# One opening, two edits: shorter weight splits on VectorE, and a first image pooled on TensorE with the averaging matrix as the stationary operand

## The chip, the cores and the metric

The kernel runs on one core of one Trainium2 chip. The metric is device time in microseconds (us) for one launch. Before the change it is 2833.58 us, the median of 3 runs (2832.46 to 2833.78).

A core has five engines that each work through their own queue in order: TensorE (PE in the profile; PEld is its weight load), VectorE (DVE), ScalarE (ACT), GpSimd (POOL) and SyncE (SP), which here only issues DMAs. Engines wait for one another through semaphores.

## The reference

```python
kv_pool = kv.reshape(B, H // 4, 4, W // 4, 4, C).mean(axis=(2, 4))   # 4x4 average
kv_flat = kv_pool.reshape(B, -1, C) @ w_sr                           # keys = values
s = (q @ kv_flat.transpose(0, 2, 1)) / np.sqrt(C)
a = np.exp(s - s.max(-1, keepdims=True))
a /= a.sum(-1, keepdims=True) + 1e-09
x = (a @ kv_flat).reshape(B * S, D)
...
h = x @ w_in
g = 0.5 * h * (1.0 + erf(h * inv_sqrt2))
return g @ w_out
```

B is 4, an image has 384 x 32 pixels of C = 128 channels, so 12288 queries and 768 keys per image; `w_in` is 128 x 2048 and `w_out` 2048 x 128. `w_in` and `w_out` come as 8-byte floats, everything else as 4-byte floats.

## The kernel before, in words

**Numbers.** TensorE multiplies in f16, and each f32 operand is split into a high f16 part and a low f16 part. A product then takes three matmuls: high by high, high by low, low by high (L558 to L560, L611 to L613, L424).

**Tiles.** The 49152 queries are 96 tiles of 512, each of 4 chunks of 128. A tile goes through `score` (6 matmuls of 384 columns a chunk), `evac` (VectorE reads the scores out of PSUM and takes the extreme), `exp` (ScalarE), `attn_hi` and `attn_lo` (VectorE makes the two f16 parts), `attn_turn` (a DMA transpose), `av` (18 matmuls), `x_out`, then 16 pairs of `mlp_in` and `gelu`, `rest` (the low f16 part `gl`), and `mlp_out`. From tile 1 on a loop (L791) emits this; tiles overlap, and each later image's keys are made inside the loop by `kv_sum`, `kv_turn` and `kv_key` (L257 to L267).

**The opening.** What stands ahead of the loop is a table written by hand, `START` (L22 to L86): a list of steps that are emitted in this order, each onto its engines' queues. It holds the loads, the keys of the first image, the splitting of the weights, tile 0 whole, and parts of tiles 1 to 3. The order of `START` is the order of every queue.

**The first image.** It comes in 12 chunks of 512 KB (`kv_load_first`, one DMA each on SP). For a chunk, `kv_add` (VectorE, L203) adds pixels 2 and 3 of each group of four onto 0 and 1; `kv_pool` (L214) finishes the average on TensorE with four matmuls: the pixels are the stationary operand (128 x 128) and `group`, the averaging matrix (128 x 32), is streamed, which gives the pooled pixels already transposed. `kv_copy` (ACT), `kv_key_first` (one matmul of 256 columns with `w_sr`, L227) and `kv_max_first` follow, three times. `kv_bound` then takes the largest value over all partitions through TensorE (`km_d`, `km_ps`, `km_m`) and ends in `kinv` (L310), with which `kv_high` and `kv_low` make the f16 keys.

**The weights.** They come in 8 blocks of 512 KB, 0 to 3 of `w_in` and 4 to 7 of `w_out`. A block is 512 eight-byte floats a partition, read as pairs of words: `up` (sign, exponent, top of the mantissa) and `low`. `w_max` takes the largest `up`, from which `w_scale` makes a scale per partition. `w_split` makes f16 high and low in five steps. Step 0 (ACT): `v` is the absolute value of `up`, `l` is `low` scaled. Step 1 (VectorE): build the f32 out of `up` (L724, L727), and zero it where the value is tiny (L730). Step 2 (ACT): the high part (L732). Step 3 (VectorE): the value's power of two (L734), times `l` (L735). Step 4 (VectorE): value times scale less high part (L738), plus scaled `l` (L739). So seven VectorE instructions a block beside `w_max`.

**Buffers.** `stage` has two buffers of two weight blocks, so `w_out` blocks load only once the `w_in` blocks in front are split. `wtmp` has four.

Of the kernel before, what the change touches and what calls it, by code (L numbers as in the profile page):

```python
# [51 lines left out]
    ("recips", 0, 3, 1), ("attn_hi", 0, 3, "dve"), ("attn_lo", 0, 3), ("attn_lo", 0, 2),
    ("attn_turn", 0, 3), ("attn_turn", 0, 2), ("score_half", 1, 2, 0), ("score_half", 1, 2, 1),
    ("w_split", 4, 0), ("evac", 1, 0), ("exp", 1, 0), ("av_first", 0, 0), ("av_first", 0, 1),
    ("evac_half", 1, 1, 0), ("evac_half", 1, 1, 1), ("exp", 1, 1), ("score", 1, 3),
    ("evac_half", 1, 2, 0), ("evac_half", 1, 2, 1), ("exp", 1, 2), ("evac", 1, 3),
    ("exp", 1, 3), ("w_max", 6), ("w_max", 7), ("av_first", 0, 3), ("av_first", 0, 2), ("x_out", 0),
    ("mlp_in", 0, 0), ("gelu", 0, 0), ("mlp_in", 0, 1), ("gelu", 0, 1),
    ("w_scale", 1, 0), ("w_scale", 1, 1), ("w_split", 4, 1), ("w_scale", 1, 2), ("out_scale",),
    ("w_split", 5, 0), ("mlp_in", 0, 2), ("gelu", 0, 2),  # L60
    ("w_split", 4, 3), ("w_split", 4, 2), ("rest", 0, 0), ("recips", 1, 0, 4),
    ("mlp_in", 0, 3), ("gelu", 0, 3), ("w_split", 4, 4), ("attn_hi", 1, 0, "act"),
    ("q_max", 2), ("q_scale", 2), ("q_split", 2), ("mlp_in", 0, 4), ("gelu", 0, 4),
    ("rest", 0, 1), ("attn_lo", 1, 0), ("attn_turn", 1, 0), ("q_turn", 2), ("q_sigma", 2),
    ("q_load", 3), ("mlp_in", 0, 5), ("gelu", 0, 5), ("w_split", 5, 1),
    ("mlp_out", 0, 0), ("mlp_in", 0, 6), ("w_split", 5, 2), ("w_split", 5, 3),
    ("rest", 0, 2), ("w_split", 6, 0),
    ("mlp_out", 0, 1), ("gelu", 0, 6), ("w_split", 3, 2), ("attn_hi", 1, 1, "act"),
    ("w_split", 5, 4), ("mlp_out", 0, 2), ("mlp_in", 0, 7), ("gelu", 0, 7), ("w_split", 3, 3),
# [26 lines left out]
def pooled_attention_mlp(  # L96
# [103 lines left out]
    def kv_add(j):  # L200

        t = st["kv0", j]
        nc.vector.tensor_tensor(t[:, :, :2], t[:, :, :2], t[:, :, 2:], op=ALU.add)  # L203
# [683 lines left out]
```

## Time and profile before

| | us |
|---|---|
| median of 3 runs | 2833.58 |
| span of the profiled execution, first to last instruction | 2831.7 |
| PE busy in it | 2786.1 (98%) |
| PEld, DVE, ACT, POOL busy | 1335.7, 2376.3, 2530.4, 845.7 |
| DMA moved | 284.90 MB, mean 101 GB/s |

The span is 1.9 us under the median; that is what lies around the first and last instruction. In the profile, a line like L214 is line 214 of the kernel before. A group's row gives its busy time and the mean of one; the text in brackets is the idle time of the engine just in front of it and the engine that ended it. PE matmuls overlap in their pipeline, so a matmul's own duration is longer than its distance to the next one. One f32 matmul instruction shows as two records.

### The profile page before, as it was taken

Reading aid. Unit: us, or ns where it says so; the run is one execution under the profiler, and the core shown is the slowest. Engines: PE = TensorE matmul, PEld = TensorE weight load, DVE = VectorE, ACT = ScalarE, POOL = GpSimd, SP = SyncE. Lnnn points to the kernel's source line nnn. Section 1 sums busy time; section 2 is a strip of 40 time slices with the busy share of each in tenths; the row PEclk is TensorE's granted clock in tenths of the full one; section 3 lists DMA queues with packets and bytes.
Section 4 is the critical chain, followed back from the end, with each engine's and each line's share of the span. In section 5 each row is a group of like instructions: output and inputs, shape, how many; then the busy total and the mean of one; then the engine's idle time right before and its main releaser. Section 6 shows DMA issues by size and latency. Waiting matters only on the chain.

```text
span 2831.7 us, 37758 instructions
## 1 busy us (share of the span) xinstructions
PE 2786.1 (98%) x13480; PEld 1335.7 (47%) x13480; DVE 2376.3 (84%) x3545; ACT 2530.4 (89%) x3416; POOL 845.7 (30%) x801
## 2 busy tenths in 40 slices
PE   6799999999999999999999999999999999999999
PEld 5344444444444444444444444444444444444444
DVE  8888888888888888888888888888888887878785
ACT  4699999899999999999999998989999999999998
POOL 1334343222233343323233443322222222222221
PEclk9899999999999999999999999999999999999999
DMA  6344454344444544343434544444443444434341
GB/s 196 86 111 102 113 118 93 89 101 90 97 105 112 119 107 110 90 97 92 101 86 111 116 105 106 110 90 97 95 97 90 96 91 92 95 92 95 91 92 49
DMA packets 852989, 284.90 MB, mean 101 GB/s; under 512 B 814656, under 2 KB 817088, under 8 KB 852800
## 3 DMA queue, kind: packets, MB, share of 16 engines
q1 hardware_dynamic: 852800, 282.49, 43.0%
q8 instruction: 105, 1.72, 0.3%
q14 instruction: 84, 0.69, 0.1%
HBM read 54.59 MB, written 25.17 MB: 28 GB/s over the span
## 4 chain that ended last, share of the span: by engine, by line
PE 93%; DVE 6%; ACT 1%; issue 0%; DMA 0%; SPq 0%; DVEq 0%; ACTq 0%
PE s L423 12%; PE px L539 12%; PE po L613 11%; PE po L612 11%; PE po L611 11%; PE h L558 11%; PE h L560 11%; PE h L559 11%; DVE gl L578 1%; DVE a L501 1%; DVE sn L434 1%; PE pp L214 1%; DVE a L497 1%; ACT sn L477 0%; DMA w<-in_moe_w_in_dram 0%
## 5 line engine op out<-in xcount | busy, mean ns | idle before, releaser
L572 ACT ACTIVATE g<-h,hs 128x512 f32<-128x512 f32 x1536 | 1005.8, 680 | 212.6 <-PE h L560 193.0
L578 DVE SCALAR_TENSOR_TENSOR gl<-g,gs,gh 128x1024 f16<-128x1024 f32 x768 | 1011.7, 1320 | 35.4 <-ACT gh L574 33.9
L574 ACT ACTIVATE gh<-g,gs 128x1024 f16<-128x1024 f32 x768 | 882.0, 1148 | 25.0
L613 PE MATMUL po<-gh,wo_l 128*128 128x512 f16 x1538 | 583.6, 380 | 5.3 <-DVE wo_l L739 5.3
L558 PE MATMUL h<-xh,wi_h 128*128 128x512 f16 x1536 | 583.1, 380 | 3.8 <-ACT g L572 2.7
L396 POOL TENSOR_TENSOR q<-q,qi 128x512 f32<-128x512 f32 x96 | 102.2, 1065 | 1614.9 <-DVE qi L388 1614.9
L612 PE MATMUL po<-gl,wo_h 128*128 128x512 f16 x1538 | 584.1, 380 | 0.1
L611 PE MATMUL po<-gh,wo_h 128*128 128x512 f16 x1538 | 584.0, 380 | 0.0
L559 PE MATMUL h<-xl,wi_h 128*128 128x512 f16 x1536 | 582.9, 379 | 0.4 <-DVE xl L550 0.4
L560 PE MATMUL h<-xh,wi_l 128*128 128x512 f16 x1536 | 582.9, 379 | 0.0
L423 PE MATMUL s<-k,q_v 128*128 128x384 f16 x2274 | 434.6, 327 | 13.4 <-DVE sn L434 7.2
L434 DVE TENSOR_SCALAR_CACHE_REDUCE sn<-s,sg 128x768 f32<-128x768 f32 x379 | 384.0, 1013 | 73.8 <-PE s L423 70.0
L501 DVE SCALAR_TENSOR_TENSOR a<-sn,r,a 128x768 f16<-128x768 f32 x384 | 408.5, 1064 | 13.5
L539 PE MATMUL px<-aT,v 128*128 128x512 f16 x1710 | 415.6, 379 | 0.2 <-issue 0.2
L477 ACT ACTIVATE sn<-sn,nm 128x768 f32<-128x768 f32 x384 | 354.5, 924 | 11.7 <-DVE sn L434 9.2
L423 PEld LDWEIGHTS <-q_v 128*128 128x128 f16 x2274 | 222.9, 98 | 204.2 <-issue 15.1
L539 PEld LDWEIGHTS <-v 128*128 128x128 f16 x1710 | 167.3, 98 | 202.2 <-issue 0.7
L497 DVE TENSOR_SCALAR a<-sn,r 128x768 f16<-128x768 f32 x377 | 248.3, 659 | 7.1 <-DVE r L493 0.5
L490 DVE TENSOR_SCALAR r<-sum 128x2 f32<-128x2 f32 (+2 forms) x192 | 39.1, 203 | 255.9 <-ACT sn L477 255.9
L613 PEld LDWEIGHTS <-wo_l 128*128 128x128 f16 x1538 | 150.9, 98 | 188.4 <-DVE wo_l L739 6.5
L560 PEld LDWEIGHTS <-wi_l 128*128 128x128 f16 x1536 | 150.5, 98 | 182.4 <-issue 1.8
L559 PEld LDWEIGHTS <-wi_h 128*128 128x128 f16 x1536 | 150.5, 98 | 181.1 <-issue 6.0
(117 smaller groups left out, 2149.1 us busy)
## 6 DMA issues: line engine op xcount, KB each, us to landing
q<-in_q_dram SPq DMA_DIRECT2D x96, 256.0 KB, 2.9
out_dram<-o SPq DMA_DIRECT2D x95, 256.0 KB, 2.0
kv<-in_kv_dram SPq DMA_DIRECT2D x72, 256.0 KB, 4.4
kv<-in_kv_dram SPq DMA_DIRECT2D x12, 512.0 KB, 9.0
aT<-a SPq DMA_TRANSPOSE x384, 3.2
w<-in_moe_w_in_dram SPq DMA_DIRECT2D x4, 512.0 KB, 6.0
w<-in_moe_w_out_dram SPq DMA_DIRECT2D x4, 512.0 KB, 5.5
q_v<-q_u SPq DMA_TRANSPOSE x96, 2.8
```

The source lines that it names most:

```text
L423: nc.tensor.matmul(ps[:, n, :KH], lhs[:, c], rhs[:, n * KH : (n + 1) * KH], start=rhs is kh and lhs is qh, stop=lhs is ql,)
L501: nc.vector.scalar_tensor_tensor(a[:, 1, :], st.pop(("s", t, c)), st["r", t][:, c : c + 1], a[:, 0, :], op0=ALU.mult, op1=ALU.subtract,)
L539: nc.tensor.matmul(ps, v[:, w, :], aT[:, :, o + k, :], start=k == 0 and i == 0, stop=k == KB - 1 and i == 2,)
L558: nc.tensor.matmul(ps, wi_h[:, fs], xh, start=True, stop=False)
L559: nc.tensor.matmul(ps, wi_h[:, fs], xl, start=False, stop=False)
L560: nc.tensor.matmul(ps, wi_l[:, fs], xh, start=False, stop=True)
L572: nc.scalar.activation(g[:, e, :], ps, AF.Gelu, scale=st["hs", b])
L574: nc.scalar.mul(gh, g, st["gs", b])
L578: nc.vector.scalar_tensor_tensor(gl, st["g", t, p], st["gs", t // TPB], st["gh", t, p], op0=ALU.mult, op1=ALU.subtract)
L611: nc.tensor.matmul(ps, wo_h[:, f, :], gh, start=f == 0, stop=False)
L612: nc.tensor.matmul(ps, wo_h[:, f, :], gl, start=False, stop=False)
L613: nc.tensor.matmul(ps, wo_l[:, f, :], gh, start=False, stop=f == FB - 1 and hi == T)
```

## The change: what it does

It has three parts.

1. **Weights.** `w_max` now has ACT take the absolute value first (`wt`) and VectorE reduce that with a clamp at `MIN64` in one instruction, so the zeroing of tiny values is gone from the split, and from `w_scale`. The split builds the f32 in place in `up` (2 VectorE instructions), GpSimd adds the scaled `low` to it (new step 2), ACT makes the high part, and one VectorE instruction makes the low part. Seven VectorE instructions become three.
2. **First image.** `kv_add` is gone. `kv_pool` runs eight matmuls a chunk in place of four; `group` is stationary now (32 columns) and the pixels are streamed (128 columns). The output has 32 partitions, and `tile_position` puts it into one of four column groups of the array, two for each chunk in turn. The result is not transposed, so a TensorE transpose and a VectorE copy (`kv_turn_first`) stand ahead of the key matmul. Copies, keys and maxima go in six pieces of 128 in place of three of 256.
3. **Order.** `START` is written anew, `stage` has 4 buffers in place of 2 and `wtmp` 8 in place of 4.

```diff
 START = [
-    ("q_load", 0), ("wi_load", 0), ("wi_load", 1), ("wi_load", 2), ("wi_load", 3), ("w_sr",),
+    ("wi_load", 0), ("q_load", 0), ("kv_load", 0), ("wi_load", 1), ("wi_load", 2), ("q_max", 0),
...
-    def kv_add(j):
-
-        t = st["kv0", j]
-        nc.vector.tensor_tensor(t[:, :, :2], t[:, :, :2], t[:, :, 2:], op=ALU.add)
-
...
+        m = P // R
+        for e in range(R):
+            for w in range(2):
+                o = ((j % 2) * 2 + w) * m
                 nc.tensor.matmul(
-                    st["pp", j // 4][:, o : o + n], t[:, w, e], group,
-                    start=e == 0, stop=e == 1,
+                    st["pp", n][o : o + m, :C], group, t[:, w, e], start=e == 0, stop=e == R - 1,
+                    tile_position=(0, o),
                 )
...
+    def kv_turn_first(n):
+        ps = ps_x.tile([P, T], F32, tag="ps_x", name=f"pt0_{n}")
+        nc.tensor.transpose(ps[:, :P], st.pop(("y", 0, n)), ident)
+        st["pT", 0, n] = prep.tile([P, P], F32, tag=f"pT{n % 2}", name=f"pT_0_{n}")
+        nc.vector.tensor_copy(st["pT", 0, n], ps[:, :P])
...
-        nc.vector.tensor_reduce(
-            st["wm", j // (DFF // WS)][:, k : k + 1], up, axis=AX.X, op=ALU.max,
-            apply_absolute_value=True,
+        st["wt", j] = wtmp.tile([P, WS], F32, tag="w", name=f"wt_{j}")
+        a = st["wt", j]
+        nc.scalar.activation(a, up, AF.Abs)
+        nc.vector.tensor_scalar(
+            a, a, MIN64, None, op0=ALU.max, op1=ALU.max,
+            accum_out=st["wm", j // (DFF // WS)][:, k : k + 1],
         )
...
         if step == 0:
-            nc.scalar.activation(v, up.bitcast(F32), AF.Abs)
-            nc.scalar.mul(l, low.bitcast(U32), 2.0**-52)
+            nc.scalar.mul(low, low.bitcast(U32), 2.0**-29)
         if step == 1:
             nc.vector.tensor_scalar(
-                ai, up, 3, 0x3FFFFFFF, op0=ALU.logical_shift_left, op1=ALU.bitwise_and
+                ai, ai, 3, 0x3FFFFFFF, op0=ALU.logical_shift_left, op1=ALU.bitwise_and
             )
             nc.vector.scalar_tensor_tensor(
-                ai, up, -0x40000000, ai, op0=ALU.bitwise_and, op1=ALU.bitwise_or
+                up, up, -0x40000000, ai, op0=ALU.bitwise_and, op1=ALU.bitwise_or
             )
-            nc.vector.scalar_tensor_tensor(v, v, MIN64, a, op0=ALU.is_ge, op1=ALU.mult)
         if step == 2:
+            nc.gpsimd.tensor_tensor(up, up, low, op=ALU.add)
+        if step == 3:
             nc.scalar.mul(hi, v, st["inv", j // (DFF // WS)])
-        if step == 3:
-            nc.vector.tensor_scalar(ai, v.bitcast(I32), -0x800000, None, op0=ALU.bitwise_and)
-            nc.vector.tensor_tensor(l, l, a, op=ALU.mult)
         if step == 4:
-            inv = st["inv", j // (DFF // WS)]
-            nc.vector.scalar_tensor_tensor(v, v, inv, hi, op0=ALU.mult, op1=ALU.subtract)
-            nc.vector.scalar_tensor_tensor(lo, l, inv, v, op0=ALU.mult, op1=ALU.add)
+            nc.vector.scalar_tensor_tensor(
+                lo, v, st["inv", j // (DFF // WS)], hi, op0=ALU.mult, op1=ALU.subtract
+            )
```

What this does to the queues is shown at three places. The first is TensorE in the pooling, before. A row is an instruction: output, then the streamed operand and the stationary one; `pp` is the pooled result, `pk` the keys, `x4` four such instructions in a row.

```order
L284 MATMUL rho_ps<-rho_d,ones 128x128
L214 MATMUL pp_0_226<-group,kv_0_146 128x32 x4
L214 MATMUL pp_0_226<-group,kv_1_148 128x32 x4
L214 MATMUL pp_0_226<-group,kv_2_150 128x32 x4
L214 MATMUL pp_0_226<-group,kv_3_152 128x32 x4
L214 MATMUL pp_1_263<-group,kv_4_154 128x32 x4
L227 MATMUL pk_0_269<-pT_0_256,w_sr_sb 128x256
```

And the same place of the changed kernel (its lines are numbered by its own file; `pt` is the new transpose of `y`):

```order
L207 MATMUL pp_0_210<-kv_0_139,group 32x128 x8
L207 MATMUL pp_0_210<-kv_1_148,group 32x128 x8
L207 MATMUL pp_1_231<-kv_2_150,group 32x128 x8
L285 MATMUL rho_ps<-rho_d,ones 128x128
L207 MATMUL pp_1_231<-kv_3_152,group 32x128 x8
L226 MATMUL pt_0_264<-ident,y_0_227 128x128
L207 MATMUL pp_2_271<-kv_4_154,group 32x128 x8
L234 MATMUL pk_0_283<-pT_0_266,w_sr_sb 128x128
```

Pooling is TensorE's first work now: the matmul for the weights' scale (`rho_ps`), which opened the queue, stands behind the third chunk, and each chunk has eight matmuls that stream 128 columns.

The second place is VectorE between the weights' scale and the first pooled chunks, before (`kv` is a chunk, `wt` and `w` weight blocks):

```order
L278 TENSOR_SCALAR rho_d<-ident,rho 128x128
L724 TENSOR_SCALAR wt_193<-w_137 128x512
L727 SCALAR_TENSOR_TENSOR wt_193<-w_137,wt_193 128x512
L730 SCALAR_TENSOR_TENSOR wt_193<-wt_193 128x512
L203 TENSOR_TENSOR kv_0_146<-kv_0_146 128x2x256
L203 TENSOR_TENSOR kv_1_148<-kv_1_148 128x2x256
L289 TENSOR_REDUCE rho_m<-rho_ps 128x1
```

In the changed kernel:

```order
L279 TENSOR_SCALAR rho_d<-ident,rho 128x128
L723 TENSOR_SCALAR wt_188<-wt_188 128x512
L726 SCALAR_TENSOR_TENSOR w_135<-w_135,wt_188 128x512
L290 TENSOR_REDUCE rho_m<-rho_ps 128x1
L700 TENSOR_SCALAR rmax<-rho_m 128x1
L701 RECIPROCAL xs<-rho_m 128x1
```

No `kv` row is left on VectorE in front of the pooling, and the third row of the split is gone.

The third place is VectorE in tile 0's MLP, around the split of the second `w_out` block, before (`a` is an attention part, `gl` the low part of the MLP's middle):

```order
L501 SCALAR_TENSOR_TENSOR a_0_660<-sn_0_496,r_649,a_0_660 128x768
L412 TENSOR_SCALAR sg_687<-qe_664,ks_360 128x4
L724 TENSOR_SCALAR wt_634<-w_183 128x512
L727 SCALAR_TENSOR_TENSOR wt_634<-w_183,wt_634 128x512
L730 SCALAR_TENSOR_TENSOR wt_634<-wt_634 128x512
L734 TENSOR_SCALAR wt_634<-wt_634 128x512
L735 TENSOR_TENSOR wt_634<-wt_634 128x512
L578 SCALAR_TENSOR_TENSOR gl_2_713<-g_4_677,gs_379,gh_4_678 128x1024
L738 SCALAR_TENSOR_TENSOR wt_634<-wt_634,inv_630,wo_h 128x512
L739 SCALAR_TENSOR_TENSOR wo_l<-wt_634,inv_630 128x512
```

In the changed kernel:

```order
L502 SCALAR_TENSOR_TENSOR a_0_723<-sn_0_572,r_720,a_0_723 128x768
L723 TENSOR_SCALAR wt_428<-wt_428 128x512
L726 SCALAR_TENSOR_TENSOR w_166<-w_166,wt_428 128x512
L579 SCALAR_TENSOR_TENSOR gl_0_762<-g_0_681,gs_449,gh_0_682 128x1024
L579 SCALAR_TENSOR_TENSOR gl_1_764<-g_2_718,gs_449,gh_2_719 128x1024
L343 TENSOR_SCALAR os_450<-hs_448,omega 128x1
L579 SCALAR_TENSOR_TENSOR gl_2_776<-g_4_741,gs_449,gh_4_742 128x1024
```

Between the attention part and the third `gl`, five rows of weight work before are two now; the two rows that ended the block (L738, L739) are one, the new L734, and it comes seven rows further on, behind GpSimd's add and ACT's high part. On GpSimd that add stands in the same queue as the three instructions that split each tile of `q`:

```order
L730 TENSOR_TENSOR w_166<-w_166 128x512
L397 TENSOR_TENSOR q_344<-q_344,qi_727 128x512
L398 CAST q_u<-q_344 128x512
L399 TENSOR_TENSOR q_u<-q_344,q_u 128x512
L730 TENSOR_TENSOR w_166<-w_166 128x512
```

Eight such adds are new there. On SP, two `w_out` loads go ahead of the last two chunks of the first image, and the first chunk goes ahead of three of the four `w_in` blocks.

More of the change, by code (lines that the diff above doesn't have):

```diff
@@ L52 @@
[L52 to L69, printed above, removed]
-    ("w_split", 3, 4), ("rest", 0, 3), ("attn_lo", 1, 1), ("attn_turn", 1, 1),
-    ("score", 2, 0), ("mlp_out", 0, 3), ("mlp_in", 0, 8), ("gelu", 0, 8), ("w_split", 6, 1),
@@ new lines @@
+    ("av_first", 0, 0), ("av_first", 0, 1), ("attn_turn", 0, 3), ("evac_half", 1, 2, 0),
+    ("evac_half", 1, 2, 1), ("score", 1, 3), ("evac", 1, 3), ("w_max", 7), ("exp", 1, 3),
+    ("w_split", 5, 0), ("av_first", 0, 3), ("exp", 1, 2), ("attn_turn", 0, 2), ("av_first", 0, 2),
+    ("x_out", 0), ("mlp_in", 0, 0), ("gelu", 0, 0), ("mlp_in", 0, 1), ("w_scale", 1, 0),
+    ("q_load", 3), ("w_split", 4, 1), ("w_split", 4, 2), ("q_max", 2), ("gelu", 0, 1),
+    ("w_scale", 1, 1), ("w_scale", 1, 2), ("w_split", 4, 3), ("mlp_in", 0, 2),
@@ new lines @@
+    ("q_scale", 3), ("q_sigma", 3), ("w_split", 5, 3), ("mlp_out", 0, 2), ("mlp_in", 0, 7),
+    ("w_split", 6, 0), ("w_split", 5, 4), ("score", 2, 0), ("mlp_out", 0, 3),
+    ("attn_hi", 1, 2, "act"), ("w_split", 3, 2), ("w_split", 3, 3), ("evac", 2, 0),
+    ("gelu", 0, 7), ("mlp_in", 0, 8), ("gelu", 0, 8), ("q_split", 3), ("w_split", 7, 0),
+    ("mlp_in", 0, 9), ("mlp_in", 0, 10), ("mlp_in", 0, 11), ("gelu", 0, 9), ("attn_lo", 1, 2),
+    ("w_split", 3, 4), ("attn_turn", 1, 2), ("w_split", 6, 1), ("rest", 0, 3), ("rest", 0, 4),
@@ new lines @@
+    ("w_split", 7, 1), ("w_split", 6, 2), ("gelu", 0, 10), ("mlp_out", 0, 4), ("mlp_out", 0, 5),
+    ("w_split", 6, 3), ("w_split", 6, 4), ("gelu", 0, 11), ("rest", 0, 5), ("mlp_in", 0, 12),
+    ("attn_hi", 1, 3, "act"), ("attn_turn", 1, 1), ("score", 2, 1), ("mlp_out", 0, 6),
+    ("mlp_in", 0, 13), ("gelu", 0, 12), ("gelu", 0, 13), ("mlp_out", 0, 7), ("attn_lo", 1, 3),
+    ("evac", 2, 1), ("attn_turn", 1, 3), ("mlp_out", 0, 8), ("mlp_in", 0, 14), ("gelu", 0, 14),
+    ("mlp_out", 0, 9), ("w_split", 7, 2), ("w_split", 7, 3), ("rest", 0, 6), ("mlp_out", 0, 10),
@@ L86 @@
+    ("mlp_out", 0, 11), ("mlp_in", 0, 15), ("score", 2, 2), ("gelu", 0, 15), ("w_split", 7, 4),
+    ("mlp_out", 0, 12), ("evac", 2, 2), ("rest", 0, 7), ("av", 1, 0), ("av", 1, 1), ("exp", 2, 2),
+    ("score", 2, 3), ("evac", 2, 3), ("av", 1, 2), ("mlp_out", 0, 13), ("mlp_out", 0, 14),
+    ("exp", 2, 0), ("exp", 2, 1), ("exp", 2, 3), ("mlp_out", 0, 15), ("q_turn", 3),
+    ("score", 3, 0), ("x_out", 1),
 ]
@@ L198, in kv_load_first @@
         st["kv0", j] = t.rearrange("p (w e c) -> p w e c", e=R, c=C)
[L200 to L203 removed]
     def kv_pool(j):
[L207 to L208 removed]
+        n = j // 2
+        if j % 2 == 0:
+            st["pp", n] = ps_h.tile([P, T], F32, tag="ps_h", name=f"pp0_{n}")
         t = st.pop(("kv0", j))
[L210 to L213 removed]
+        m = P // R
@@ L238, in kv_sum_part, with kv_key_first @@
+    def kv_key_first(n):
+        if n == 0:
+            st["kT", 0] = prep.tile([P, KEYS], F32, tag="kT", name="kT_0")
+        st["pk", n] = ps_o.tile([P, T], F32, tag="ps_o", name=f"pk0_{n}")
+        nc.tensor.matmul(
+            st["pk", n][:, :P], w_sr_sb, st.pop(("pT", 0, n)), start=True, stop=True
+        )
+        nc.scalar.copy(st["kT", 0][:, n * P : (n + 1) * P], st["pk", n][:, :P])
     def kv_sum_part(b, h, i, eng):
```

124 lines of the change are left out of this document (52 added, 72 removed).

## The prediction

> **What bounds the kernel now.** I read the profile's totals first, then the busy time of each engine by stage, cutting the span where VectorE's and TensorE's rows show a step.
>
> ```profile
> PE 2786.1 (98%) x13480; PEld 1335.7 (47%) x13480; DVE 2376.3 (84%) x3545; ACT 2530.4 (89%) x3416; POOL 845.7 (30%) x801
> ```
>
> ```profile
> core 0: us, PE busy (x) PEld busy (x) DVE busy (x) ACT busy (x) POOL busy (x), PEclk, DMA share, GB/s
> 14.50:38.20 23.70, 22.96 (x100) 22.12 (x100) 20.80 (x40) 3.30 (x8) 2.14 (x3) 1.00 0.66 238
> 38.20:42.80 4.60, 2.02 (x4) 1.03 (x5) 2.83 (x11) 0.37 (x1) 1.43 (x1) 1.00 0.88 259
> 42.80:63.10 20.30, 16.55 (x120) 10.73 (x120) 19.48 (x58) 12.76 (x24) 0.00 (x0) 0.92 0.53 117
> 63.10:114.90 51.80, 37.33 (x147) 15.52 (x147) 47.45 (x79) 35.27 (x50) 8.80 (x6) 0.87 0.20 46
> 114.90:134.30 19.40, 14.83 (x64) 6.54 (x63) 18.09 (x28) 13.68 (x17) 6.71 (x5) 0.91 0.71 154
> 134.30:2800.00 2665.70, 2663.97 (x12914) 1266.43 (x12913) 2245.40 (x3301) 2434.21 (x3279) 818.83 (x773) 1.00 0.43 99
> ```
>
> From 134.3 on TensorE is busy 2663.97 of 2665.70 us, and the change leaves the instructions there as they are. So only the moment at which the loop starts can move, and the end moves with it. Ahead of that are three stages. Pooling (14.5 to 38.2) is TensorE's, with VectorE at 20.80 of 23.70. Attention of tile 0 (42.8 to 63.1) is VectorE's: 19.48 of 20.30. Tile 0's MLP (63.1 to 114.9) is VectorE's again, 47.45 of 51.80, while TensorE, busy 37.33, waits in between. Their borders are these rows of the timelines of VectorE and TensorE: the reciprocal that the keys wait for, the first rows of `x_out` for tile 0, the first `mlp_in` of tile 1.
>
> ```profile
> 42.60 0.16 DVE L310 RECIPROCAL kinv<-kap 128x1 f32<-128x1 f32 x1
> 63.06 0.74 DVE L549 TENSOR_SCALAR xh<-px,xs 128x512 f16<-128x512 f32 x1
> 114.86 0.38 PE L558 MATMUL h<-xh,wi_h 128*128 128x512 f16 x1
> ```
>
> So before: 42.6 us to `kinv` (A), 20.5 to `xh` (B), 51.8 to tile 1 (C). A change has to be costed in each.
>
> **The change, part by part. C, the weights.** These are VectorE's groups inside C that belong to the split, and the attention group that runs beside GpSimd there.
>
> ```profile
> L501 DVE SCALAR_TENSOR_TENSOR a<-sn,r,a 128x768 f16<-128x768 f32 x4 | 5.7, 1430 | 0.0
> ...
> L735 DVE TENSOR_TENSOR wt<-wt 128x512 f32<-128x512 f32 x5 | 3.7, 749 | 0.2
> L727 DVE SCALAR_TENSOR_TENSOR wt<-w,wt 128x512 int32<-128x512 int32 x4 | 3.6, 900 | 0.1
> L739 DVE SCALAR_TENSOR_TENSOR wo_l<-wt,inv 128x512 f16<-128x512 f32 x4 | 3.0, 752 | 0.1
> L734 DVE TENSOR_SCALAR wt<-wt 128x512 int32<-128x512 int32 x5 | 3.0, 590 | 0.0
> L738 DVE SCALAR_TENSOR_TENSOR wt<-wt,inv,wo_h 128x512 f32<-128x512 f32 x4 | 2.9, 737 | 0.0
> L730 DVE SCALAR_TENSOR_TENSOR wt<-wt 128x512 f32<-128x512 f32 x4 | 2.8, 692 | 0.2
> L724 DVE TENSOR_SCALAR wt<-w 128x512 int32<-128x512 int32 x4 | 1.7, 419 | 0.0
> ```
>
> These are 3.7 + 3.6 + 3.0 + 3.0 + 2.9 + 2.8 + 1.7 = 20.7 us; the last `w_in` block's L738 and L739, a group each of their own, add 1.5 by the same means: 22.2. What stands there afterwards is four shifts (0.42 each, as L724), four merges (like L727) and five low parts (0.75, as L739). Alone, a merge takes 0.69, and an attention part 1.01, as these two answers show (VectorE's timeline at 18 us, and its groups from 43 to 63.1, where GpSimd is idle):
>
> ```profile
> 18.46 0.69 DVE L727 SCALAR_TENSOR_TENSOR wt<-w,wt 128x512 int32<-128x512 int32 x1
> ```
>
> ```profile
> L501 DVE SCALAR_TENSOR_TENSOR a<-sn,r,a 128x768 f16<-128x768 f32 x4 | 4.0, 1011 | 0.2
> ```
>
> So 1.7 + 2.8 + 3.8 = 8.3. In C the same instructions are longer while GpSimd splits `q`: 4 x 0.42 at L501, 4 x 0.21 at L727, 5 x 0.17 at L734, 5 x 0.06 at L735, together 3.7 us for GpSimd's 8.80, or 0.42 a us. The 2.0 of it that lay on split rows falls on other rows now. The added GpSimd work is one add a block, five of them in C. The nearest rows are GpSimd's own `q` products on 128x512 f32, 1.83 on average from 46 to 140 us, beside a busy VectorE, and 1.04 for the first of all:
>
> ```profile
> L396 POOL TENSOR_TENSOR q<-q,qi 128x512 f32<-128x512 f32 x3 | 5.5, 1826 | 77.1 <-DVE qi L388 77.1
> ```
>
> ```profile
> 4.99 1.04 POOL L396 TENSOR_TENSOR q<-q,qi 128x512 f32<-128x512 f32 x1 [3.59 <-DVE qi L388]
> ```
>
> At 1.5 each, five adds cost VectorE 7.5 x 0.42 = 3.1 us (bounds 2.2 and 3.9). VectorE's work in C becomes 47.45 - 22.2 + 8.3 + 2.0 + 3.1 - 0.2 (the dropped tiny instruction of `w_scale`) = 38.5. Its idle time was 4.35; I keep that: each block has one handoff more (through GpSimd), but VectorE has other rows in its queue to fill it. C is 42.8, 9.0 less. ScalarE's 35.27 only falls, since three `Abs` go ahead of C, so it doesn't bind; nor does TensorE's 37.33, part of it at half rate.
>
> **B.** Same work, one split instruction less ahead of the first `evac` (0.75, L738) and one of three `w_max` earlier (0.67). The new `w_max` is a clamp with an accumulator, for which the trace has this shape at 384 elements out of PSUM (groups of the same window):
>
> ```profile
> L466 DVE TENSOR_SCALAR_CACHE_REDUCE sn<-s,sg 128x384 f32<-128x384 f32 x10 | 5.7, 610 | 0.0
> ...
> L661 DVE TENSOR_REDUCE wm<-w 128x1 f32<-128x512 f32 x3 | 1.9, 674 | 0.0
> ```
>
> Scaled from 0.61 to 512 elements that is about 0.8 against 0.67, so 0.1 to 0.2 more for each of two. B gains 1.2. Its `Abs` is hidden: ScalarE is busy 12.76 of 20.30.
>
> **A, the pooling.** Removed: twelve additions on VectorE, and the wait for the first.
>
> ```profile
> 14.50 8.74 PE L214 MATMUL pp<-group,kv 128*128 128x32 f32 x40 [1.60 <-DVE kv L203]
> ```
>
> That row is 20 instructions, so 0.43 us each, and 48 of them are 20.6 us. They stream 32 columns only; the weight load sets the pace (22.12 of 23.70 busy). Afterwards 96 instructions stream 128 columns each. The nearest row is a key matmul of just that form in the steady part of the chain:
>
> ```profile
> 195.62 0.22 PE pk L266 x2
> ```
>
> 0.22 each, with the weight load hidden, at full rate. In the opening TensorE is slower: its weight-load timeline has a load every 0.32 us for matmuls of 384 columns there, against 0.97 for six (0.16) later.
>
> ```profile
> 45.94 0.15 PEld L454 LDWEIGHTS <-q_v 128*128 128x128 f16 x1 [0.17 <-issue]
> 46.26 0.15 PEld L454 LDWEIGHTS <-q_v 128*128 128x128 f16 x1 [0.17 <-issue]
> ```
>
> ```profile
> 151.13 0.97 PE s L423 x6
> ```
>
> So 23 us of busy pooling left TensorE at half rate, whatever the column PEclk says (1.00). The Trainium skill ("TensorE: Matmul & The Clock Gate", Part 1) has the half rate as the default, lifted by about 3.4 us of sustained activity; the trace disagrees, unless waiting for weights does not count as activity. By that rule the new pooling, which streams all the time, would cost 0.22 an instruction after its start; by the trace as it stands, 0.43.
>
> Upwards, then: 96 x 0.43 = 41 us. Downwards, the arrival of the pixels: chunks are 512 KB, issued from 4.0 to 15.7 us and landed 8 to 10 us later, so the last at about 25.
>
> ```profile
> L197 SPq DMA_DIRECT2D kv<-in_kv_dram x12: 328/328/782, 4.0 to 15.7; - x12
> ...
> DMA to landing us min/median/max: 8.0/9.0/10.0
> ```
>
> ```profile
> 12.00:16.00 4.00, 2.27 (x9) 2.01 (x10) 3.79 (x10) 0.72 (x1) 0.00 (x0) 1.00 1.03 421
> ```
>
> At 421 GB/s a chunk takes 1.25 us. The new order puts two `w_out` blocks (1.05 MB) ahead of the last two chunks and one `q` tile (0.26 MB) behind, so the last lands 1.9 us later, at 27. Successive matmuls of a chunk write two different column groups and share neither weights nor outputs. If they overlap in pairs, a chunk takes 8 x 0.22 / 2 = 0.9 us and its share of transpose and key matmuls 0.2 to 0.4: it keeps pace with the DMA, and pooling ends at 28. No matmul of this trace uses fewer than 128 columns, so that isn't shown; I take it because the bound by arrival holds over a wide span of costs (up to 0.12 an instruction, and at 0.16 it is late by some 3 us only). Then the tail: from the last pooled copy (37.80) to `kinv` (42.60) were 4.8 us; the transpose, its copy and one more handoff add some 1.2. `kinv` comes at 34.2, 8.4 earlier.
>
> ```profile
> 37.80 0.37 ACT L221 COPY pT<-pp 128x256 f32<-128x256 f32 x1 [4.83 <-PE pp L214]
> ```
>
> Behind VectorE's waits for those transposes nothing urgent queues: two splits and two low parts, which tile 0 needs only at C. On SP the transpose of tile 0's `q` now stands behind that `q` tile and a third `w_out` block (0.52 MB), so it starts at about 28.5.
>
> ```profile
> q_v<-q_u SPq DMA_TRANSPOSE x96, 2.8
> ```
>
> It lands 3 to 5 us later, just under `kinv`; if it is late, by 1 us or so, and the forecast's range carries that.
>
> **Sum.** 8.4 + 1.2 + 9.0 = 18.6. The profiled span, 2831.7, becomes 2813.1; with the 1.9 between span and median (2833.58) that is 2815.
>
> **The rivals.** (1) *Column groups don't overlap, full rate.* The first weight block reaches VectorE at 5.49 before:
>
> ```profile
> 5.49 0.69 DVE L661 TENSOR_REDUCE wm<-w 128x1 f32<-128x512 f32 x1 [0.59 <-DMA w<-in_moe_w_in_dram]
> ```
>
> Seven instructions of 0.2 to 0.7 now stand between that and `group`, so pooling starts at about 9.2. Eight instructions at 0.43 end at 12.6, the second chunk at 16, then 80 x 0.22 = 17.6 and ten small matmuls at 0.25: 36. With the longer tail `kinv` comes at 42, and A gains nothing. 2833.6 - 10.2 = 2823. For it: every row here is serial. Against it: the layout of the writes. The Trainium skill ("TensorEngine Tiling (Array Packing)", Key Properties) says that different tiles run weight loads and matmuls in parallel, and that a change of tiling mode drains TensorE; by its first half the time is 2815, and no run so far shows either.
>
> (2) *Slower: serial and at half rate.* Pooling takes 41 us on top of 9.2 and ends, with the small matmuls, at 55; `kinv` at 61 is 18.6 late, B and C give back 10.2, and the time is 2842. It decides from about 0.35 us an instruction, where `kinv` is late by the 10.2 that B and C give back. For it: the half rate in the rows above. Against it: streaming is denser than before.
>
> (3) *GpSimd's adds become the wait.* The add for the second `w_out` block stands behind a whole split of `q` (L396 to L398, 8.80 / 2 = 4.4 us a tile); ScalarE's high part waits for it, and the GELUs queue behind that on ScalarE, then TensorE. Two such waits of 4.4 take C's gain: 2833.6 - 9.6 = 2824.
>
> (4) *More than the sum.* VectorE's 4.35 of idle in C goes, and tile 1 (18.09 of 19.40 busy) starts with less behind it, some 2 us: 2809.
>
> **How the numbers follow.** Forecast 0.48, (1) 0.24, (2) 0.06, (3) 0.12, (4) 0.10. The range 2808 to 2826 holds all but (2) and the edges of the rest. 0.2% is 5.7 us, about what a measurement here tells from no change: faster than 2827.9 is 0.89, slower than 2839.3 is 0.06, between 0.05.
>
> **What would show it.** Right: pooling ends near 28 and `kinv` stands near 34; `xh` comes 19 later and tile 1's first matmul 43 after that; split rows on VectorE are three a block. Wrong in A: a pooled instruction takes over 0.2, and TensorE is busy without a gap until 36 or later. Wrong in C: ScalarE's high part waits for GpSimd's add (new L730), or VectorE's idle time in C passes 10 us. Wrong altogether: the stretch behind tile 1 no longer has TensorE at 99.9%.

## The result and the profile after

The changed kernel takes 2816.95 us, the median of 4 runs (2815.68 to 2818.09), beside 2833.68 (2832.46 to 2833.90) for the kernel before. The ratio is 0.9942, with a 95% interval of 0.9928 to 0.9955. The forecast was 2815. Its profiled execution has a span of 2816.3 and took 2818.1 as a whole. Between experiments below, medians move by about 1 us from one set of runs to the next, so what is under 2 us is read from the places in the profile, not from the times.

First the same three marks as before: the reciprocal for the keys, the first `x_out` row, and tile 1's first `mlp_in`, from the timelines of VectorE and TensorE of the changed kernel (its lines stand one further down).

```profile
37.40 0.16 DVE L311 RECIPROCAL kinv<-kap 128x1 f32<-128x1 f32 x1
57.67 0.75 DVE L550 TENSOR_SCALAR xh<-px,xs 128x512 f16<-128x512 f32 x1 [0.70 <-PE px L526]
100.10 0.38 PE L559 MATMUL h<-xh,wi_h 128*128 128x512 f16 x1
```

Stage A ends at 37.40 instead of 42.60, 5.2 earlier (forecast 8.4). B takes 20.27 instead of 20.46, 0.2 less (forecast 1.2). C takes 42.43 instead of 51.80, 9.4 less (forecast 9.0). What follows takes 2716.2 instead of 2716.8. Together 15.4, the difference of the two spans. The busy times of each engine by these stages, and behind tile 1:

```profile
core 0: us, PE busy (x) PEld busy (x) DVE busy (x) ACT busy (x) POOL busy (x), PEclk, DMA share, GB/s
0.00:37.40 37.40, 19.89 (x214) 15.03 (x215) 18.56 (x61) 12.63 (x26) 9.89 (x16) 0.90 0.90 311
37.40:57.70 20.30, 15.48 (x120) 9.60 (x120) 18.43 (x59) 12.52 (x23) 0.28 (x1) 0.85 0.56 123
57.70:100.10 42.40, 31.52 (x147) 13.96 (x146) 38.89 (x62) 34.99 (x50) 16.53 (x11) 1.00 0.22 50
...
134.00:2800.00 2666.00, 2664.10 (x12912) 1266.18 (x12911) 2237.85 (x3291) 2436.38 (x3277) 816.96 (x766) 1.00 0.43 99
```

The loop is TensorE's as before, 2664.10 of 2666.00. C is still VectorE's: 38.89 of 42.40, where the forecast had 38.5 of 42.8. GpSimd's 16.53 are 8.2 of `q` splits and 8.3 of five new adds. In A no engine is near full, but the DMA share is 0.90: the pooling now waits for pixels. TensorE's timeline of that stage shows how:

```profile
9.44 1.92 PE L207 MATMUL pp<-kv,group 128*32 128x128 f32 x16 [9.44 <-DVE group L169]
...
19.28 2.02 PE L207 MATMUL pp<-kv,group 128*32 128x128 f32 x48
...
23.28 1.07 PE L207 MATMUL pp<-kv,group 128*32 128x128 f32 x16
28.19 1.92 PE L207 MATMUL pp<-kv,group 128*32 128x128 f32 x16 [3.85 <-DMA kv<-in_kv_dram]
...
30.88 1.92 PE L207 MATMUL pp<-kv,group 128*32 128x128 f32 x16
```

One chunk is eight matmuls, 16 records. Three chunks in a row take 2.02, so 0.67 a chunk and 0.084 a matmul (e10 below tests whether the alternation makes it so). Ten chunks are pooled by 24.4. Then TensorE waits 3.85 us for the eleventh, which stood behind two `w_out` blocks, and takes 1.92 for each of the last two, as long as for the very first chunk.

### The profile page after: what moved, and what is told of

Its sections match the earlier page's. It is cut to its first block, busy times and chain, and to the rows that moved or that the text cites. A ratio compares the mean times of both kernels' runs of the same rounds, so it can differ in the third digit from the quotient of the medians.

```text
span 2816.3 us, 37971 instructions
## 1 busy us (share of the span) xinstructions
PE 2773.4 (98%) x13588; PEld 1324.2 (47%) x13588; DVE 2348.0 (83%) x3516; ACT 2533.9 (90%) x3422; POOL 859.8 (31%) x809
## 4 chain that ended last, share of the span: by engine, by line
PE 92%; DVE 5%; DMA 1%; ACT 1%; issue 0%; SPq 0%; DVEq 0%; ACTq 0%
PE s L424 13%; PE px L540 12%; PE po L613 11%; PE po L614 11%; PE po L612 11%; PE h L559 11%; PE h L561 11%; PE h L560 11%; DVE gl L579 2%; DVE a L502 1%; DMA kv<-in_kv_dram 1%; DVE a L498 1%; DVE sn L435 1%; ACT sn L478 0%; ACT L478 0%
## 6 DMA issues: line engine op xcount, KB each, us to landing
w<-in_moe_w_out_dram SPq DMA_DIRECT2D x4, 512.0 KB, 11.1
```

## Twelve experiments

Each kernel is told by its edit, with the expectation that was written down ahead of it. The ratio is to the kernel before, which took 2832.84 to 2833.61 in these runs. The marks are those of the profile, one execution each: end of A, length of B, length of C. Three kernels share one opening but for a single step (changed, e11, e12), and A ends in them between 37.01 and 37.40.

| kernel | A ends | B | C | median us | ratio, 95% interval |
|---|---|---|---|---|---|
| before | 42.60 | 20.46 | 51.80 | 2833.68 | |
| changed | 37.40 | 20.27 | 42.43 | 2816.95 | 0.9928 to 0.9955 |
| e1 split alone | 42.62 | 23.78 | 47.91 | 2831.61 | 0.9983 to 1.0001 |
| e2 pooling and order alone | 37.39 | 22.78 | 51.60 | 2828.98 | 0.9975 to 0.9993 |
| e3 pixels first | 36.27 | 20.19 | 42.34 | 2814.23 | 0.9919 to 0.9944 |
| e4 filler matmuls | 35.69 | 20.11 | 42.38 | 2816.64 | 0.9924 to 0.9949 |
| e5 = e1, add on VectorE | 43.38 | 23.90 | 47.43 | 2833.30 | 0.9989 to 1.0007 |
| e6 = e1, `w_max` earlier | 41.76 | 20.96 | 47.43 | 2828.42 | 0.9973 to 0.9991 |
| e7 = changed, add on VectorE | 36.71 | 20.05 | 44.35 | 2819.38 | 0.9933 to 0.9958 |
| e8 = e3, tail cleared | 32.07 | 21.98 | 42.42 | 2815.22 | 0.9922 to 0.9947 |
| e9 = e6, new order in C | 41.55 | 20.55 | 42.36 | 2822.29 | 0.9949 to 0.9974 |
| e10 = changed, grouped | 36.66 | 20.27 | 42.33 | 2816.13 | 0.9927 to 0.9955 |
| e11 = changed, old order in C | 37.30 | 20.94 | 47.05 | 2823.73 | 0.9954 to 0.9979 |
| e12 = e11, two adds earlier | 37.01 | 20.75 | 44.52 | 2820.49 | 0.9942 to 0.9969 |

**The split alone (e1).** The kernel before, with the new `w_max`, `w_scale` and `w_split`; its steps take the places of the old ones.

```diff
-stage ... bufs=2      wtmp ... bufs=4
+stage ... bufs=4      wtmp ... bufs=8
-("w_split", j, 1)     ("w_split", j, 2)     ("w_split", j, 3)
+("w_split", j, 1), ("w_split", j, 2)     ("w_split", j, 3)     (nothing)
```

> Only the weight split of the change, in the old pooling and the old order (a split's new second and third step stand where its old second stood). Theory (C is VectorE's own work, the split rows alone pay there): the stretch from the first x_out row to tile 1's first mlp_in falls by about 9 us from 51.8, pooling and attention stay within 1 us, and the time is 2833.6 - 9.5 = 2824, 2822 to 2826. Rival (the new order pays in C, because GpSimd's adds eat what the shorter split saves): C falls by less than 4 us and the time is 2830 or more.

The theory fell: C lost 3.9, not 9, B grew by 3.3, and the time is 2831.61, which is not told apart from no change. The rival's numbers came, but not its reason, adds that eat what the split saves: VectorE's work did fall. This is the wait of VectorE for ScalarE in B, and the busy times of C, where it works 36.40 us (11.1 less than before) and idles 11.5 of 47.90:

```profile
DVE wt L658 <- ACT wt L657: 3.5, 2, 1.8
```

```profile
66.40:114.30 47.90, 35.77 (x146) 15.34 (x146) 36.40 (x60) 32.98 (x47) 15.06 (x10) 0.89 0.23 50
```

So the work is gone, 11.1 of it where 9.0 were reckoned, but waits took its place. In B the new `w_max` waits twice for ScalarE's `Abs`, which stands behind the keys' high part and behind the exponentials. The waits in C are taken apart below.

**Pooling and order alone (e2).** The changed kernel with the old seven-row split (and old `w_max`, `w_scale`); step 4 also does the old step 3.

```diff
-if step == 2: nc.gpsimd.tensor_tensor(up, up, low, op=ALU.add)
+if step == 4: (the old steps 3 and 4)
-stage ... bufs=4      wtmp ... bufs=8
+stage ... bufs=3      wtmp ... bufs=4, three words a value
```

> Only the pooling and the new order of the opening, with the old weight split: VectorE's seven rows a block as before. Theory (the two edits act on different stages and add up): kinv near 37.5 instead of 42.6, C as long as before or up to 2 us longer, the time 2833.6 - 5.2 = 2828.4, 2826 to 2830. Rival (VectorE's old rows fill the shortened pooling stage, so that the pooled keys wait for it): kinv past 40 and the time above 2831.

A ends at 37.39, C is 51.60 and the time 2828.98, all as the theory had them. B is 2.3 longer than before, which nobody had expected: the last four rows of an old split stand between the first mark and the low parts of the keys, which start 2.6 us behind the mark instead of 0.9. In C the new order by itself is worth nothing. The split by itself is worth 3.9 there, both together 9.4.

**Pixels first (e3) and filler (e4).** Two tests of what ends A.

```diff
+("kv_load", 10), ("kv_load", 11),
 ("wo_load", 0), ("wo_load", 1),
-("kv_load", 10), ("kv_load", 11),
...
-("w_max", 4), ("kv_copy", 4), ... ("kv_copy", 5),
+("kv_copy", 4), ... ("kv_copy", 5), ("w_max", 4),
```

> The whole change, with the last two pixel chunks issued ahead of the two w_out blocks, and w_max of the first of these blocks behind the last pooled copy. Theory (in the pooling stage the arrival of the last chunks decides): they land 2.5 us earlier (1.05 MB at 0.41 MB a us), TensorE's wait of 3.85 us at 24.3 shrinks to under 1.5, kinv stands near 34.5 to 35, and the time is 2817 - 2.7 = 2814.3. Rival (the half rate and the chain of transposes and maxima behind the last chunk decide, or tile 0's q transpose, which lands at the end of this stage, becomes the wait): under 1 us, 2816 to 2817.5.

```diff
 ("kv_pool", 9),
+("warm", 14),        # 14 x matmul(ps[:, :P], ident, ident)
 ("kv_pool", 10),
```

> The whole change, with 14 matmuls of the identity with itself (f32, 128 columns, 0.22 us each at full rate, results unused) between the tenth and the eleventh pooled chunk, where TensorE otherwise waits 3.85 us. Theory (the idle gap drops the clock to half, and that costs the last two chunks and their tail some 2 us): both chunks take about 1.0 instead of 1.92 us, kinv comes 1.5 to 2 us earlier, 2815.2. Rival (the last two chunks wait for the DMA alone and the clock does not matter): kinv within 0.5 us, 2817. If the filler itself runs at half rate it ends late, and kinv comes 1 to 2.5 us later.

In e3 the eleventh chunk is pooled 2.5 us earlier, as computed, but the first mark moves by 1.1 only. TensorE's row for that chunk, two of VectorE's behind it, and TensorE's next key matmul:

```profile
25.71 1.07 PE L205 MATMUL pp<-kv,group 128*32 128x128 f32 x16 [0.98 <-DMA kv<-in_kv_dram]
```

```profile
30.39 0.69 DVE L374 TENSOR_REDUCE qm<-q 128x4 f32<-128x512 f32 x1 [2.16 <-DMA q<-in_q_dram]
...
31.59 0.28 DVE L226 COPY pT<-pt 128x128 f32<-128x128 f32 x1
```

```profile
32.13 0.80 PE L232 MATMUL pk<-pT,w_sr_sb 128*128 128x128 f32 x2 [3.12 <-DVE mx L217]
```

Pooling is over at 28.3, but the maximum of tile 1's `q` stands on VectorE ahead of the last copy and waits for its own DMA, and the first `w_out` block's `w_max` follows. The arrival was the limit, and a wait next to it took over. The time, 2814.23, is what the theory said, but not by its sum: of the 3.5 us between the two profiled spans (2816.3 and 2812.8) only 1.3 stand ahead of tile 1, and the rest, behind it, was not taken apart. In e4 the same chunks, still late, run at full rate:

```profile
24.32 3.39 PE L213 MATMUL warm<-ident 128*128 128x128 f32 x28
...
28.34 1.07 PE L205 MATMUL pp<-kv,group 128*32 128x128 f32 x16 [0.62 <-DMA kv<-in_kv_dram]
...
29.82 1.07 PE L205 MATMUL pp<-kv,group 128*32 128x128 f32 x16
```

The stretches around that gap (the clock that TensorE was granted is the number behind POOL's), in the changed kernel and then in e4:

```profile
26.00:28.00 2.00, 0.00 (x0) 0.00 (x0) 0.69 (x2) 0.80 (x3) 0.00 (x0) 0.65 1.03 401
28.00:30.00 2.00, 1.81 (x16) 1.50 (x16) 0.00 (x0) 0.00 (x0) 0.00 (x0) 0.50 1.91 281
30.00:32.00 2.00, 2.00 (x17) 1.58 (x17) 1.44 (x4) 0.27 (x1) 0.00 (x0) 0.50 0.61 156
```

```profile
26.00:28.00 2.00, 1.71 (x16) 1.52 (x14) 0.69 (x2) 1.00 (x3) 0.00 (x0) 1.00 1.01 397
28.00:30.00 2.00, 1.66 (x23) 1.37 (x25) 0.30 (x2) 0.07 (x1) 0.00 (x0) 1.00 1.96 284
30.00:32.00 2.00, 1.61 (x19) 1.05 (x15) 1.77 (x5) 0.72 (x3) 0.00 (x0) 1.00 0.46 125
```

So the wait of 3.85 us halves the clock, and work without use that fills it keeps the clock up; the first mark comes 1.7 earlier, as the theory had it. The Trainium skill ("TensorE: Matmul & The Clock Gate", Part 1) has the half rate return after an idle window of about 3.4 us. Here less was enough: 0.65 over 26 to 28, if the clock fell once from 1.00 to 0.50, puts the fall at 26.6, some 2.2 us after TensorE's last matmul, and in e3 the key matmul behind a wait of 3.12 us takes 0.80 instead of 0.49. The time, 2816.64, is too near the changed kernel's to show the 1.7.

**The tail cleared (e8).** Its edit, against e3:

```diff
 ("kv_load", 11),
+("q_load", 1),
 ("wo_load", 0), ("wo_load", 1),
...
-("kv_copy", 5), ("w_max", 4), ... ("kv_bound", 1), ("w_max", 5), ("kv_bound", 2),
+("kv_copy", 5), ... ("kv_bound", 1), ("w_max", 4), ("kv_bound", 2), ("w_max", 5),
```

> e3_pixels_first with the chain behind the last chunk cleared: tile 1's q is loaded right behind the last chunk (its maximum stood ahead of that chain on VectorE and waited 2.16 us for its data), and w_max of blocks 4 and 5 stand behind the keys' bound instead of ahead of it. Theory (the chain from the last pooled copy to kinv is 4.6 us when nothing stands in it): kinv near 33.2 instead of 36.27, B 1.4 longer at most for the moved rows, the time 2814.2 - 2 = 2812, 2811 to 2813. Rival (B cannot start earlier, since tile 0's q transpose lands later than the keys): B grows by all that A loses, 2814.

The first mark is at 32.07, 5.3 before the changed kernel's, better than the 33.2 expected. The rival, that B would grow by all that A loses, fell: A ends 4.2 earlier than in e3, and B is 1.8 longer than in e3: block 5's `w_max` (0.75) now lies in it, the low parts of the keys run beside GpSimd's split of `q` (2.39 for the two, 1.15 in e3), and the first score meets the wait that the rival named:

```profile
33.27 0.82 PE L422 MATMUL s<-k,q_v 128*128 128x384 f16 x2 [2.12 <-DMA q_v<-q_u]
```

Tile 1 starts at 96.47, 3.6 earlier than in the changed kernel and 2.3 earlier than in e3, but most of the lead over e3 is lost behind that mark: the profiled spans are 2812.1 and 2812.8. The medians, 2815.22 and 2814.23 beside 2816.95, do not tell the three apart, and the theory's 2811 to 2813 did not come. These two are the best of all the runs, by an amount that the timing cannot show.

**Grouped (e10).** Does the overlap of column groups matter?

```diff
-for e in range(R):
-    for w in range(2):
+for w in range(2):
+    for e in range(R):
```

> The whole change, with the two loops of the pooling exchanged: four matmuls in a row accumulate in the same column group, where the change alternates between two. Theory (it is the alternation that overlaps two column groups): a chunk takes 1.75 us instead of 1.07 while warm, and the last two, at half rate, 3.4 each instead of 1.92; kinv comes 2 to 3 us later than 37.40, and the time is 2819. Rival (a matmul into a group of 32 columns is short by itself, in whatever order): chunks of 1.0 to 1.1 us, kinv within 0.5 of 37.40, and 2817.

Three chunks in a row, and the last two, on TensorE:

```profile
21.63 3.39 PE L207 MATMUL pp<-kv,group 128*32 128x128 f32 x48
...
27.47 2.46 PE L207 MATMUL pp<-kv,group 128*32 128x128 f32 x32
...
30.34 1.53 PE L207 MATMUL pp<-kv,group 128*32 128x128 f32 x16
```

A chunk takes 1.13 in place of 0.67, so alternation does overlap the work of two column groups; whether it is the weight loads, the streams or both that overlap was not told apart. The Trainium skill ("TensorEngine Tiling (Array Packing)", Key Properties) says that different tiles run weight loads and matmuls in parallel, and this agrees. But both expectations on the mark were wrong: it comes 0.7 earlier, at 36.66. The slower pooling is still busy when the eleventh chunk lands, and keeps its full rate (granted 1.00 in every stretch from 22 to 32). So the speed of the pooling was not what ended A.

**Where the add runs (e5, e7).** The second step on VectorE, in e1 and in the changed kernel.

```diff
-nc.gpsimd.tensor_tensor(up, up, low, op=ALU.add)
+nc.vector.tensor_tensor(up, up, low, op=ALU.bitwise_or)
```

> The weight split alone in the old order (as e1_weights), with its second step on VectorE instead of GpSimd, as a bitwise OR (the same but for a carry out of the lowest three bits). In e1_weights ScalarE waited 9.0 us for two GpSimd adds in the stretch C (x_out to tile 1), and VectorE idled 11.5 of its 47.9 us. Theory (the hop through GpSimd, where an add stands behind a split of q, is what cost the gain): VectorE has 5 x 0.75 more and little idle, C is 44 to 45 us, the time 2828.5. Rival (the old order itself sets merge and high part too close, on whatever engine the step stands): C stays at 47 to 49 us, the time 2831 to 2833.

> The whole change with the split's second step on VectorE instead of GpSimd, as a bitwise OR (the same but for a carry out of the lowest three bits). Theory (GpSimd's adds cost VectorE 3.1 us of contention in C, as forecast, and spare it five rows of 0.70): C stays within 1 us of 42.4 and the time is 2816 to 2818. Rival a (the adds on GpSimd are nearly free): C is 45 to 46 and the time 2820. Rival b (contention and the waits behind GpSimd cost more than forecast): C is under 41 and the time 2814 or less.

In e5 the rival held: C is 47.43, hardly better than with the add on GpSimd (47.91). VectorE works 2.0 more there and idles 2.5 less, and ScalarE's high part still waits 5.2 for VectorE's own row. So the hop to GpSimd is at most a part of what costs the gain in the old order. In e7 the result lies between the theory and rival a: C is 44.35, 1.9 longer:

```profile
56.76:101.11 44.35, 34.70 (x146) 15.01 (x146) 39.55 (x67) 35.12 (x50) 7.45 (x6) 0.88 0.21 48
```

Five rows of 0.86 were added, 4.3, but VectorE's busy time in C rose only from 38.89 to 39.55; so the adds on GpSimd cost its other rows 3.6 (forecast 3.1). The rest of the 1.9 is idle time, 1.3 more. VectorE's groups in C of the changed kernel show where that falls:

```profile
L579 DVE SCALAR_TENSOR_TENSOR gl<-g,gs,gh 128x1024 f16<-128x1024 f32 x8 | 13.1, 1654 | 0.0
...
L734 DVE SCALAR_TENSOR_TENSOR wo_l<-w,inv,wo_h 128x512 f16<-128x512 f32 x4 | 3.6, 902 | 0.2 <-ACT wo_h L732 0.2
L723 DVE TENSOR_SCALAR wt<-wt 128x512 int32<-128x512 int32 x4 | 3.6, 895 | 0.0
L726 DVE SCALAR_TENSOR_TENSOR w<-w,wt 128x512 int32<-128x512 int32 x4 | 2.8, 693 | 0.1
```

Beside GpSimd `gl` takes 1.65 on average where e7 has 1.28, the shift 0.90 where it has 0.66; the merge takes 0.69 in both.

**`w_max` earlier (e6).**

```diff
 ("kv_bound", 2),
+("w_max", 5),
 ("kv_high", 0), ("kv_high", 1),
-("w_max", 5),
...
+("w_max", 6), ("attn_lo", 0, 3), ... ("w_max", 7), ("exp", 1, 1), ... ("exp", 1, 3),
-("attn_lo", 0, 3), ... ("exp", 1, 1), ... ("exp", 1, 3), ("w_max", 6), ("w_max", 7),
```

> e1_weights with three of the new w_max calls moved earlier: block 5's ahead of the high part of the keys, block 6's and 7's ahead of the low parts and exponentials of the attention stage, so that ScalarE's Abs has run when VectorE comes to the clamp. In e1_weights VectorE waited 1.80 and 1.70 us for these, and the stretch B (kinv to xh) was 23.8 us. Theory (the new handoff to ScalarE is free only where the order gives it a lead): B falls to 20.5 and the time by 3.3, to 2828.3. Rival (another wait follows in C): B falls, C grows by as much, and the time stays within 1 us of 2831.6.

As the theory had it, B falls to 20.96 and the time to 2828.42. A clamp that follows its `Abs` too closely waits 1.7 to 1.8 us each time, and 0.4 at most in e6, where the order gives it a lead. A ends 0.9 earlier too, which was not taken apart.

**The order inside C (e9, e11).** Both exchange the part of `START` from tile 0's `x_out` on: e9 puts the new one behind e6, e11 the old one behind the new opening. One or two steps of a split change sides with it: in e11 block 3's add stands ahead of `x_out`, so C holds four adds and not five.

```diff
 (all entries ahead of ("x_out", 0) as in e6; in e11 as in the changed kernel)
-("x_out", 0), ... (as in e6; in e11 as in the changed kernel)
+("x_out", 0), ... (as in the changed kernel; in e11 as in e6)
```

> e6_weights_early_max (old pooling, old opening, new split) with the steps from tile 0's x_out on in the changed kernel's order. C was 47.4 us in e6, with the add on GpSimd, and 47.4 in e5, with it on VectorE, against 42.4 in the changed kernel. Theory (the order inside C, which stands the merge, the add and the high part of a block apart, is what lets the shorter split pay): C is 42.4 to 43.5 and the time 2828.4 - 4.9 = 2823.5, 2822.5 to 2825. Rival (what the new opening leaves for C, or when it starts, decides): C stays above 46 and the time at 2827 or more.

> The converse of e9: the whole change, with the steps from tile 0's x_out on in the order of the kernel before. Theory (the order inside C decides): kinv and xh as in the changed kernel (37.4 and 57.7), C 47 to 48 us, the time 2817 + 5 = 2822, 2821 to 2823.5. Rival (the opening decides): C under 44 and the time 2816 to 2818.5.

Both as the theory had them: C is 42.36 and 47.05. The order of the steps in C is worth 4.6 to 5.1 us to the new split, and 0.2 to the old one. Where VectorE waits in C, in e11 and then in the changed kernel:

```profile
DVE gl L577 <- ACT gh L573: 4.0, 4, 1.8
DVE wo_l L732 <- ACT wo_h L730: 2.5, 2, 1.7
DVE xh L548 <- PE px L538: 1.9, 1, 1.9
DVE wi_l L732 <- ACT wi_h L730: 1.0, 1, 1.0
```

```profile
DVE sn L435 <- PE s L424: 2.4, 1, 2.4
DVE xh L550 <- PE px L526: 0.7, 1, 0.7
...
DVE wo_l L734 <- ACT wo_h L732: 0.2, 1, 0.2
```

In e11 it waits 7.5 us for ScalarE, in the changed kernel 0.2. Block 5, and in the last two rows block 7, show the mechanism, on VectorE, GpSimd and ScalarE of e11, in order of time:

```profile
70.11 1.28 POOL L397 TENSOR_TENSOR q_u<-q,q_u 128x512 f16<-128x512 f32 x1
70.42 1.52 DVE L724 SCALAR_TENSOR_TENSOR w<-w,wt 128x512 int32<-128x512 int32 x1
...
72.09 1.95 POOL L728 TENSOR_TENSOR w<-w 128x512 int32<-128x512 int32 x1 [0.69 <-DVE w L724]
74.07 0.75 ACT L730 ACTIVATE wo_h<-w,inv 128x512 f16<-128x512 f32 x1 [4.73 <-POOL w L728]
...
74.85 0.75 DVE L732 SCALAR_TENSOR_TENSOR wo_l<-w,inv,wo_h 128x512 f16<-128x512 f32 x1 [1.71 <-ACT wo_h L730]
75.28 0.66 ACT L571 ACTIVATE g<-h,hs 128x512 f32<-128x512 f32 x1
...
91.98 1.68 POOL L728 TENSOR_TENSOR w<-w 128x512 int32<-128x512 int32 x1 [2.29 <-DVE w L724]
93.70 0.76 ACT L730 ACTIVATE wo_h<-w,inv 128x512 f16<-128x512 f32 x1 [3.28 <-POOL w L728]
```

The merge comes late on VectorE, behind tile 2's `q`, and beside GpSimd's split of that `q` it takes 1.52 instead of 0.69. The add waits for the merge, not for the split, which has ended: GpSimd stands idle for 0.69, and for 2.29 at block 7. Beside VectorE's `gl` the add takes 1.95 instead of 1.04. ScalarE has nothing ahead of the high part, so it stands still for 4.73, and the next GELU, and then VectorE's `gl`, with it. In the changed kernel the same block's high part comes as ScalarE's turn comes, without a wait; one later block still waits:

```profile
67.38 0.69 DVE L726 SCALAR_TENSOR_TENSOR w<-w,wt 128x512 int32<-128x512 int32 x1
...
68.22 3.93 POOL L730 TENSOR_TENSOR w<-w 128x512 int32<-128x512 int32 x2 [1.15 <-DVE w L726]
...
70.20 0.77 ACT L732 ACTIVATE wo_h<-w,inv 128x512 f16<-128x512 f32 x1
...
83.06 0.76 ACT L732 ACTIVATE wo_h<-w,inv 128x512 f16<-128x512 f32 x1 [4.61 <-POOL w L730]
```

**Two adds earlier (e12).** Is that wait the whole of it?

```diff
+("w_split", 5, 1), ("w_split", 5, 2),
 ("q_max", 2), ("q_scale", 2), ("q_split", 2),
...
-("w_split", 5, 1), ("w_split", 5, 2),
...
+("w_split", 7, 0), ("w_split", 7, 1), ("w_split", 7, 2),
 ("evac", 2, 0), ("q_max", 3),
...
-("w_split", 7, 0), ... ("w_split", 7, 1), ("w_split", 7, 2),
```

> e11_old_order_in_c with five entries moved: the merge and the GpSimd add of block 5 ahead of tile 2's q (maximum, scale and split), and the low part, merge and add of block 7 ahead of tile 3's q. In e11 ScalarE's high part waited 4.73 and 3.28 us for just these two adds, which stood behind a split of q on GpSimd, and the GELUs queued behind it; C was 47.05 us there and 42.4 in the changed kernel. Theory (rival 3 of the prediction is real, and the changed kernel's order is what avoids it): both waits fall under 1 us, C is 42.5 to 44 and the time 2823.7 - 4 = 2819.7, 2818.5 to 2821.5. Rival (other places of the old order cost it): the waits go, C stays above 45.5, and the time above 2822.

The two waits are gone, C falls from 47.05 to 44.52, a little above the theory's 44, and the time to 2820.49. That is 2.5 of 4.6. The waits of ScalarE in C that are left in e12 are others:

```profile
ACT g L571 <- DVE sn L433: 6.5, 1, 6.5
ACT sn L476 <- DVE sn L433: 3.7, 1, 3.7
```

So the merges and adds of two blocks, standing behind a tile's `q`, are over half of what the old order costs. The other 2.1 us, in which waits for tile 2's `evac` stand out, were not taken apart.

## Why the prediction was right, and where not

**The whole.** 2815 against 2816.95: the likeliest case came, and the three stages are the ones that moved. The gain was put at 18.6 and is 16.7 by the medians. By the two profiled spans it is 15.4: A fell short by 3.2 and B by 1.0, C was 0.4 better than its term, and 0.6 came behind tile 1, which had no term. The profiled run is the slowest of the four; that the median lies 1.1 below it is luck, not part of the sum.

**A, the term that was mis-sized.** Its mechanism held: the column groups overlap (e10), at 0.67 a chunk where 0.9 was reckoned, and pooling keeps up with the DMA. What failed is the step from "the last lands 1.9 us later, at 27" to "pooling ends at 28". TensorE could take up the eleventh chunk only at 28.19, and the twelfth, issued at 19.7 with 9.6 us to landing, came at about 29.3. The 25 that the 27 starts from was low by the prediction's own rows: 15.7 for the last issue and up to 10.0 to landing make 25.7. And the eleventh's issue alone took 3.2 us on SP, where a chunk's took at most 0.8 before. So two chunks were left to do, not one; and the wait of 3.85 us halved the clock for both, which the prediction had not thought of. Pooling ended at 32.8. That is 4.8 late, of which the clock is 1.9 (30.9 in e4) and the rest the arrival. The chain behind it, 4.6 from there to the mark, was shorter than the 6.2 reckoned. The prediction named the `w_out` blocks ahead of the last chunks and costed them by bytes alone; what they cost TensorE through its idle time was left out.

**B.** The work fell as costed, from 19.64 to 18.43, but VectorE's idle time rose from 0.8 to 1.9: it now waits 0.8 for scores, which TensorE still begins at half rate (weight loads 0.32 apart at a granted 0.50), and 0.7 for `px`. The step that failed is "same work, ... B gains 1.2", which took B to be VectorE's alone. "Its `Abs` is hidden" holds only where the order gives it a lead (e1 against e6).

**C.** The sum held: 38.89 busy against 38.5, idle 3.5 against 4.35, and the adds cost VectorE's other rows 3.6 against 3.1. Single rows did not: the four shifts, put at 0.42 each, take 0.90. What the prediction did not see is that "I keep that: ... VectorE has other rows in its queue to fill it" is a statement about the new order. In the old one the same split leaves 11.5 idle (e1) and gains 3.9. Of rival (3), the high part that waits for the add while GELUs queue behind it is real, at 4.73 and 3.28 us in e11, and gone in e12. But the add did not wait for the split of `q` on GpSimd, as (3) had it; it waited for the merge, which stood late on VectorE, and with the add on VectorE the high part waits as well (5.2 in e5). The changed kernel keeps a single such wait, the 4.61 at 83.06, for which VectorE did not wait. The prediction priced this rival as something the change might bring, where it is what the third edit had to avoid. By the medians, each good to about 1 us, step by step from the kernel before: the split alone 2.1 us, three `w_max` earlier 3.2, the order in C 6.1, the pooling and its opening 5.3, together 16.7.

**The other rivals.** (1) and (2) fall: a matmul costs 0.084 and not 0.22 or 0.43, and 0.24 at half rate (1.92 / 8). Even without overlap it is 0.14 (1.13 / 8), and A is no longer for it. The half rate of (2) was read from scores 0.32 us apart, and they do not show it: in e4 the last chunks run at a granted 1.00, and behind waits of up to 1.85 us the scores are 0.32 apart again. What speaks for half rate in the old pooling is its key matmuls, whose two weight loads take 0.50 to 0.55 where e4 takes 0.30 at a granted 1.00. (4) falls too: VectorE's idle time in C stayed, 3.5 of 4.35.
